# Seven twice-split products with other buffers and another order of their side work, in a gated mix of local attention and a GeGLU layer

## The chip, the cores and the metric

The kernel runs on one core of one Trainium2 chip. The metric is the device time of one execution in microseconds (us). Three executions of the kernel before took 753.84, 754.22 and 755.27 us; the median is 754.22. One more execution was taken with the hardware profiler on.

The core's engines run side by side, each through its own queue of instructions: TensorE (PE in the profile) multiplies matrices into eight banks of PSUM, VectorE (DVE) and ScalarE (ACT) work elementwise and can read and write PSUM, GpSimd (POOL) and SyncE (SP) mostly issue transfers (DMAs) here. PEld is PE's loading of weights.

## The reference

The input x has 2048 tokens of 1024 numbers (bfloat16). Two layers read it, and a gate per token mixes them:

```python
g = sigmoid((x * gate_w).sum(-1, keepdims=True))
a = attention(x, wqkv) @ wo          # 32 heads of 32, each token sees 8 tokens, 2 apart
b = (gelu(x @ w_gate) * (x @ w_up)) @ w_down      # 3584 hidden columns
return g * a + (1 - g) * b
```

## The kernel before, in words

The kernel splits its large matrix products by Strassen's method in Winograd's form: a product of two 2 by 2 block matrices is made from seven block products instead of eight, for some additions of blocks. An order written out by hand sets every engine's queue: inside `tc.manual_schedule` each engine runs its instructions in the order in which the program issues them, and the framework adds the semaphore waits that data, buffers and PSUM banks need.

The change lies in the last stage, after about 514 us. There the two output projections are one product. The hidden columns h of the GeGLU layer, times 1 - g, and the attention's output o, which already carries g, are laid side by side along the contraction: 28 tiles of h and 8 of o, each 128 deep, make 36. `w_down` and `wo` are stacked likewise. For each half s of the tokens (s = 0 and 1, 1024 tokens each) the left matrix A has two chunks of 512 tokens and two halves of the contraction of 18 tiles (`NK`); the right matrix R has two halves of the contraction and two halves of the 1024 output columns. A block is 18 tiles of 128 by 512, 18 KB in each partition. `R_BUF` cuts the arena in SBUF into ten buffers of that size; `plan[s]` gives each named block its buffer, and a buffer is used again and again.

The seven block products of one s, in the order of PE's queue (`down`), are P1 = A11 R11, P2 = A12 R21, P5 = S T1, P6 = S2 T2, P3 = (A12 - S2) R22, P7 = (A11 - A21) T3 and P4 = A22 T4, with S = A21 + A22 and S2 = A22 - (A11 - A21). The blocks T1 to T4 are differences of the weights, made earlier and kept in device memory (`t_d`). An A block is loaded (`load_A`), its h tiles are multiplied by 1 - g on DVE (`scale_task`, L894), and the sums are made there (`comb_task`, L901, five additions for a block). The difference A11 - A21 is written over A11, S2 over A21.

PE makes a plain block product with 72 matmuls of 512 columns (`mm`, L1015). Seven of the fourteen are split a second time (`level2`, matmuls L990 of 256 columns, 126 for a product): P5, P6 and P7 of s = 0, and P1, P5, P6 and P7 of s = 1. Such a product needs eight "forms" on DVE (`forms_L`, L959, and `forms_R`, L967, four each, written into two buffers named L5, R5 and so on), and consists of seven sub-products, each for two banks. Its four banks are XT (6, 7, 0, 1) or VT (2, 3, 4, 5), two groups of four. The sub-products add onto what stands in the banks, so the left halves are filled with zeros first (`zero_left`, L979, DVE). Between sub-products ScalarE copies half banks (L995): after the first one from one bank to another, before the second adds onto the same bank; after the third into float32 space `p5d` that lies behind the three right forms in their buffer. Ahead of the last sub-product DVE adds `p5d` to the right halves (L1003, the inner additions), first to the last two banks, then to the first two:

```python
            prod(0, 1, lf[:, 3], rq(1, 1))
            for i in (1, 0):
                TT(out=two_banks(bk, i, 1), in0=two_banks(bk, i, 1), in1=p5d, op=ALU.add)
            prod(1, 0, lq(1, 1), rf[:, 2])
```

After P1, four copies on ScalarE take its banks to `u2` (L1034, or L1048 and L1050 for s = 0); after P2 four take the first output (L1057); after P5 four take its banks to `qs` (L1066). After P6 DVE makes sums from the banks, `u2` and `qs` (L1074 and L1075); the other outputs are made by `add_out` (L1024), and `emit` sends each (L1020) by Pool's queue or, at the very end, SP's. The loads are issued on SP's queue, which holds a load until its buffer is free.

The last stage begins while the stage before it ends. PE starts P1 of s = 0 with the tiles that are there. The h tiles of A11 and A12 that come from the last two pairs of hidden columns are loaded by themselves, in `pre_down_3`, after Pool has stored these pairs to device memory (`h_store`, L256). SP then loads A21 (`loads(0, "A21")`), A22, T1 and T2.

Of the kernel before, what the change touches and what calls it, by code (L numbers as in the profile page):

```python
# [9 lines left out]
ALU = mybir.AluOpType  # L10
# [57 lines left out]
def kernel(  # L68
# [64 lines left out]
    with tc.manual_schedule(engines={mybir.EngineType.PE, mybir.EngineType.DVE, mybir.EngineType.Activation,  # L133
# [55 lines left out]
        def flat(a):  # L189
            return a.rearrange("p a b -> p (a b)")  # L190
# [609 lines left out]
        bufs = [reg3(R_BUF[k], NK, SC) for k in range(10)]  # L800
        NH_ = NPAIR

        def load_A(b, s, half, c, i0, i1, with_o):
            t0 = s * SUP + c * SC
            nc.sync.dma_start(out=b[:, i0:i1, :], in_=h_src(half, t0, i0, i1))
            if with_o:
                nc.sync.dma_start(out=b[:, NH_:NK, :], in_=o_d[:, half * 4:half * 4 + 4, t0:t0 + SC])

        def h_src(half, t0, i0, i1):
            return h_d[:, :, t0:t0 + SC].rearrange("p (i two) s -> p i two s", two=2)[:, i0:i1, half, :]  # L810
# [51 lines left out]
        def tf_close():  # L862
            while tf_open[0] and not tft.done:
# [4 lines left out]

        at_end(TFE - 1, tf_close)

        plan = [dict(A11=4, R11=5, A12=2, R21=3, A21=6, A22=0, S=8, T1=1, T2=9, L5=7, R5=5, L6=3, R6=1,
                     R22=7, T3=5, T4=8, L7=3, R7=1),
                dict(A11=6, R11=9, L1=2, R1=7, A12=4, R21=5, A21=3, A22=0, S=8, T1=1, T2=9, L5=2, R5=7, L6=5, R6=1,
                     R22=7, T3=2, T4=8, L7=5, R7=1)]
        u2 = regf(R_U2, 4 * SC).rearrange("p (j n) -> p j n", j=4)
        qs = regf(R_QS, 4 * SC).rearrange("p (j n) -> p j n", j=4)
        on = [0]
# [53 lines left out]
        def pre_down_3(s):  # L931
            B = Bs(s)
            for k, half in (("A11", 0), ("A12", 1)):
                load_A(B[k], s, half, 0, NE_, NH_, False)

        def loads(s, *names):
            B = Bs(s)
# [36 lines left out]
        def two_banks(bk, i, h):  # L974
            return banks[:, bk[2 * i]:bk[2 * i] + 2, h * HN:(h + 1) * HN]

        def zero_left(bk):
            for i in range(2):
                V.memset(two_banks(bk, i, 0), 0.0)  # L979

        def level2(bk, L, R, lf, rf):
            p5d = flat(rf)[:, 3 * KH * HN:3 * KH * HN + 4 * HN].bitcast(F32).rearrange("p (j n) -> p j n", j=2)
            lf, rf = quads(lf), quads(rf)
            lq, rq = lambda r, c: quarter(L, c, r), lambda r, c: quarter(R, r, c)
            c = lambda i, h, j: banks[:, bk[2 * i + j], h * HN:(h + 1) * HN]

            def prod(i, h, l, r, then=None):
                for j in range(2):
                    for kt in range(KH):
                        nc.tensor.matmul(c(i, h, j), lhsT=l[:, kt, j * P:(j + 1) * P], rhs=r[:, kt, :], start=False,  # L990
                                         stop=(kt == KH - 1), skip_group_check=True)
                    if then:
                        then(j)

            cp = lambda d, s_: nc.scalar.copy(out=d, in_=s_)  # L995
            prod(0, 0, lq(0, 0), rq(0, 0), lambda j: cp(c(1, 1, j), c(0, 0, j)))
            prod(0, 0, lq(0, 1), rq(1, 0))
            prod(1, 0, lf[:, 0], rf[:, 0], lambda j: cp(p5d[:, j, :], c(1, 0, j)))
            prod(1, 1, lf[:, 1], rf[:, 1], lambda j: cp(c(0, 1, j), c(1, 1, j)))
            prod(1, 1, lf[:, 2], rq(0, 1), lambda j: cp(c(1, 0, j), c(1, 1, j)))  # L1000
            prod(0, 1, lf[:, 3], rq(1, 1))
            for i in (1, 0):
                TT(out=two_banks(bk, i, 1), in0=two_banks(bk, i, 1), in1=p5d, op=ALU.add)  # L1003
            prod(1, 0, lq(1, 1), rf[:, 2])

        def down(s):
            B = Bs(s)
            last = s == 1
            eng = nc.gpsimd
            base = s * SUP  # L1010
            XT, VT = (6, 7, 0, 1), (2, 3, 4, 5)

            def mm(ps, L, R, j, start, q0=0, q1=NK):
                for q, i in list(enumerate(KORD))[q0:q1]:
                    nc.tensor.matmul(ps, lhsT=L[:, i, j * P:(j + 1) * P], rhs=R[:, i, :], start=(start and q == 0),  # L1015
                                     stop=(q == NK - 1), skip_group_check=not start)

            def emit(ot, c, nh, j):
                r0 = base + c * SC + j * P
                (nc.sync if last and (c, nh) == (1, 0) else eng).dma_start(out=o2[r0:r0 + P, nh * SC:(nh + 1) * SC], in_=ot)  # L1020

            def add_out(ps, t_, c, nh, j):
                ot = out_tile()
                TT(out=ot, in0=ps, in1=t_, op=ALU.add)  # L1024
                emit(ot, c, nh, j)

            A11, A12, A21, A22, S = B["A11"], B["A12"], B["A21"], B["A22"], B["S"]
            XP = [bank(XT[j]) for j in range(4)]
            VP = [bank(VT[j]) for j in range(4)]
            if last:  # L1030
                run(scale_task(A12, s, 0, 0, NE_))
                level2(XT, A11, B["R11"], B["L1"], B["R1"])
                for j in range(4):
                    nc.scalar.copy(out=u2[:, j, :], in_=XP[j])  # L1034
                loads(s, "T2")
                run(scale_task(A21, s, 1, 0, NE_))
            else:
                rest = scale_task(A21, s, 1, 0, NE_)
                for j in range(4):
                    if j > 1:  # L1040
                        mm(XP[j], A11, B["R11"], j, True)
                    else:
                        mm(XP[j], A11, B["R11"], j, True, 0, NK - 2)
                        yield
                        if j == 1:
                            for jj in range(2):
                                mm(XP[jj], A11, B["R11"], jj, True, NK - 2, NK)
                                nc.scalar.copy(out=u2[:, jj, :], in_=XP[jj])  # L1048
                    if j > 1:
                        nc.scalar.copy(out=u2[:, j, :], in_=XP[j])  # L1050
                    take(rest, 3)
                run(rest)
            run(comb_task(A11, A11, A21, ALU.subtract), scale_task(A22, s, 1, 0, NE_), comb_task(S, A21, A22, ALU.add))
            for j in range(4):
                mm(XP[j], A12, B["R21"], j, False)
                ot = out_tile()
                nc.scalar.copy(out=ot, in_=XP[j])  # L1057
                emit(ot, 0, 0, j)
            zero_left(VT)
            run(woven(forms_L(B["L5"], S), forms_R(B["R5"], B["T1"])))  # L1060
            run(comb_task(A21, A22, A11, ALU.subtract))
            S2 = A21
            zero_left(XT)
            level2(VT, S, B["T1"], B["L5"], B["R5"])
            for j in range(4):
                nc.scalar.copy(out=qs[:, j, :], in_=VP[j])  # L1066
            loads(s, "R22", "T3", "T4")
            run(woven(forms_L(B["L6"], S2), forms_R(B["R6"], B["T2"])))
            run(comb_task(A12, A12, S2, ALU.subtract))
            level2(XT, S2, B["T2"], B["L6"], B["R6"])  # L1070
            if not last:
                loads(1, "A11", "R11")
            for j in range(4):
                TT(out=u2[:, j, :], in0=XP[j], in1=u2[:, j, :], op=ALU.add)  # L1074
                TT(out=qs[:, j, :], in0=qs[:, j, :], in1=u2[:, j, :], op=ALU.add)  # L1075
            zero_left(XT)
            rest = woven(forms_L(B["L7"], A11), forms_R(B["R7"], B["T3"]))
            for j in range(4):
                mm(VP[j], A12, B["R22"], j, False)
                take(rest, 2)  # L1080
                add_out(VP[j], u2[:, j, :], 0, 1, j)
            run(rest)
            rest = pieces()
            if not last:
                N = Bs(1)
                run(scale_task(N["A11"], 1, 0, 0, NE_))
                rest = woven(forms_L(N["L1"], N["A11"]), forms_R(N["R1"], N["R11"]))
                take(rest, 2)
            level2(XT, A11, B["T3"], B["L7"], B["R7"])
            if not last:  # L1090
                loads(1, "A12", "R21", "A21", "T1")
            for j in range(4):
                add_out(XP[j], qs[:, j, :], 1, 1, j)
                TT(out=u2[:, j, :], in0=XP[j], in1=u2[:, j, :], op=ALU.add)
            if not last:
                zero_left(XT)
            for j in range(4):
                mm(VP[j], A22, B["T4"], j, True)
                take(rest, 2)
                add_out(VP[j], u2[:, j, :], 1, 0, j)  # L1100
            if not last:
                loads(1, "A22")
            run(rest)

        n = len(units)
        at(n - 16, lambda: load_R(Bs(0)["R11"], 0, 0))
# [73 lines left out]
```

## Time and profile before

| what | us |
|---|---|
| executions, median (lowest to highest) | 754.22 (753.84 to 755.27) |
| the profiled execution | 755.15 |
| its span, first to last instruction | 753.3 |
| PE busy in the span | 722.1 (96%) |
| DVE busy | 661.3 (88%) |
| ScalarE busy | 310.6 (41%) |
| Pool busy | 116.9 (16%) |
| mean granted clock of PE | 0.986 |

A busy PE is not PE at its peak; what a stage can win is read from PE's idle time there and from what ended it. The last stage by PE's timeline, start of each block product in us of the span:

| s | P1 | P2 | P5 | P6 | P3 | P7 | P4 | end |
|---|---|---|---|---|---|---|---|---|
| 0 | 516.5 (with gaps) | 543.4 | 559.24 | about 576.3 | 592.81 | 608.35 | 622.11 | 637.8 |
| 1 | 637.65 | 651.40 | 668.87 | about 688.3 | 704.81 | 720.35 | 734.10 | 749.8 |

In the tables of the profile, L followed by a number is a line of the kernel, an engine's name is followed by its operation and by the tile that it writes and the one that it reads, and a bracket gives the idle time before the instruction and the instruction or transfer that ended it.

### The profile page before, as it was taken

The page shows a single profiled execution, that of the slowest core. Times are in us where ns is not written, and L with a number is a line of the kernel's source. Part 1 is how long each engine was busy: PE and PEld are TensorE (multiplying, and loading weights), DVE is VectorE, ACT ScalarE, POOL GpSimd, SP SyncE. Part 2 cuts the span into 40 slices and gives each one's busy share as a digit, 9 for nine tenths or more (in the row PEclk, how much of TensorE's full clock was granted, in tenths as well). Part 3 has the DMA queues.
Part 4 walks back from the last instruction along what each step waited for, and adds up shares of the span by engine and source line. Part 5 has one row for each costly group of instructions (what it writes and reads, how often), then busy time and mean ns, then how long its engine had stood idle before and what let it go on. Part 6 is the DMA issues. An engine that isn't in the chain of part 4 may idle for free.

```text
span 753.3 us, 10346 instructions
## 1 busy us (share of the span) xinstructions
PE 722.1 (96%) x3945; PEld 394.5 (52%) x3945; DVE 661.3 (88%) x716; ACT 310.6 (41%) x556; POOL 116.9 (16%) x208
## 2 busy tenths in 40 slices
PE   8999999999999999999999999998698999997998
PEld 4466565555544444444444444443257675765673
DVE  3699999969998999999999999996399989699953
ACT  4544445445575755555555555552112010222010
POOL 1233435211201401011010000001010002000010
PEclk9999999999999999999999999999799999998999
DMA  9976864572337945345247652617966839932701
GB/s 279 265 213 223 259 198 145 211 233 84 105 93 223 364 149 161 123 140 170 84 155 228 195 170 71 208 57 245 361 273 219 320 117 319 384 135 97 288 22 57
DMA packets 119602, 143.92 MB, mean 191 GB/s; under 512 B 18897, under 2 KB 103025, under 8 KB 118529
## 3 DMA queue, kind: packets, MB, share of 16 engines
q1 hardware_dynamic: 105664, 102.58, 42.2%
q0 software_dynamic: 13600, 40.16, 15.7%
q8 instruction: 31, 0.51, 0.3%
q10 hardware_dynamic: 288, 0.52, 0.2%
q14 instruction: 19, 0.15, 0.1%
HBM read 101.16 MB, written 39.99 MB: 187 GB/s over the span
## 4 chain that ended last, share of the span: by engine, by line
PE 58%; DVE 15%; DMA 5%; issue 1%; ACT 1%; SPq 0%; DVEq 0%; ACTq 0%
PE banks L362 44%; PE banks L1015 9%; DVE arena L901 5%; PE banks L990 4%; DMA arena<-h_d 4%; DVE arena L967 3%; DVE arena L959 3%; DVE arena L894 1%; DMA arena<-in_B_w_down_dram 1%; DVE arena L593 1%; DVE arena L399 1%; DVE banks L979 1%; DVE banks L1003 0%; PE banks L598 0%; DVE arena L644 0%
## 5 line engine op out<-in xcount | busy, mean ns | idle before, releaser
L362 PE MATMUL banks<-arena 128*128 128x512 bf16 x2184 | 475.4, 379 | 4.8 <-DVE arena L399 3.0
L362 PEld LDWEIGHTS <-arena 128*128 128x128 bf16 x2184 | 240.5, 111 | 239.1 <-issue 11.0
L1015 PE MATMUL banks<-arena 128*128 128x512 bf16 x504 | 112.1, 384 | 8.6 <-DMA arena<-h_d 8.6
L990 PE MATMUL banks<-arena 128*128 128x256 bf16 x882 | 101.7, 279 | 11.6 <-DVE banks L1003 9.8
L399 DVE TENSOR_TENSOR arena<-banks,arena 128x1024 bf16<-128x1024 f32 x78 | 95.3, 1221 | 18.8 <-PE banks L362 11.7
L990 PEld LDWEIGHTS <-arena 128*128 128x128 bf16 x882 | 88.2, 100 | 25.6 <-issue 12.5
L385 ACT COPY arena<-banks 128x512 f32<-128x512 f32 x78 | 45.8, 587 | 130.8 <-PE banks L362 130.8
L1015 PEld LDWEIGHTS <-arena 128*128 128x128 bf16 x504 | 49.7, 99 | 68.8 <-DMA arena<-h_d 9.1
L370 ACT CAST arena<-banks 128x512 bf16<-128x512 f32 x102 | 59.8, 586 | 43.8 <-PE banks L362 43.8
L739 DVE TENSOR_TENSOR arena<-arena 128x2048 bf16<-128x2048 bf16 x64 | 77.1, 1220 | 0.5
L593 DVE TENSOR_TENSOR arena<-arena 128x2048 bf16<-128x2048 bf16 x64 | 74.8, 1219 | 0.1
L746 DVE TENSOR_TENSOR arena<-arena 128x2048 bf16<-128x2048 bf16 (+2 forms) x96 | 73.9, 776 | 1.0
L256 POOL DMA_DIRECT2D h_d<-arena x28 | 20.0, 716 | 251.5 <-DVE arena L252 205.2
L392 ACT COPY banks<-banks 128x512 f32<-128x512 f32 x78 | 44.5, 571 | 23.9 <-PE banks L362 18.1
L995 ACT COPY banks<-banks 128x256 f32<-128x256 f32 x42 | 15.0, 357 | 87.9 <-PE banks L990 87.9
L380 ACT COPY banks<-banks 128x512 f32<-128x512 f32 x78 | 45.0, 577 | 13.8 <-PE banks L362 12.7
L1020 POOL DMA_DIRECT2D out_dram<-arena x28 | 15.2, 543 | 197.6 <-DVE arena L1024 137.3
L901 DVE TENSOR_TENSOR arena<-arena 128x2048 bf16<-128x2048 bf16 (+1 forms) x40 | 41.9, 1120 | 0.0
L319 DVE TENSOR_TENSOR arena<-arena 128x1024 bf16<-128x1024 bf16 x60 | 38.7, 686 | 0.5
L894 DVE TENSOR_TENSOR arena<-arena,omgrep 128x2048 bf16<-128x2048 bf16 x24 | 27.9, 1221 | 12.2 <-DMA arena<-h_d 12.2
L368 ACT ACTIVATE arena<-banks 128x512 bf16<-128x512 f32 x54 | 32.3, 597 | 15.4 <-PE banks L362 15.4
L252 DVE TENSOR_TENSOR arena<-arena 128x2048 bf16<-128x2048 bf16 x28 | 34.1, 1217 | 5.0 <-ACT arena L370 3.7
(85 smaller groups left out, 441.4 us busy)
## 6 DMA issues: line engine op xcount, KB each, us to landing
arena<-t_d SPq DMA_DIRECT2D x8, 2304.0 KB, 14.6
h_d<-arena POOLq DMA_DIRECT2D x28, 512.0 KB, 4.0
arena<-in_B_w_down_dram SPq DMA_DIRECT2D x6, 1792.0 KB, 12.6
arena<-h_d SPq DMA_DIRECT2D x6, 1792.0 KB, 12.8
t_d<-arena POOLq DMA_DIRECT2D x36, 256.0 KB, 4.1
arena<-in_B_w_down_dram SPq DMA_DIRECT2D x32, 256.0 KB, 5.5
arena<-in_B_w_gate_dram SPq DMA_DIRECT2D x15, 512.0 KB, 5.4
arena<-in_B_w_up_dram SPq DMA_DIRECT2D x15, 512.0 KB, 4.5
```

Source lines behind the costliest of these rows:

```text
L362: self.pe = nc.tensor.matmul(ps, lhsT=self.L[form](kt), rhs=rhs[:, kt, :], start=(start and kt == 0), stop=(kt == HK - 1), skip_group_chec ...
L370: nc.scalar.copy(out=o_, in_=i_)
L380: nc.scalar.copy(out=self.Y, in_=self.X)
L385: nc.scalar.copy(out=self.p5s, in_=self.V)
L392: nc.scalar.copy(out=self.Z, in_=self.Y)
L399: TT(out=self.T[:, :, c2s], in0=pair, in1=self.p5s.rearrange("p (o n) -> p o n", o=1).to_broadcast([P, 2, SC]), op=ALU.add)
L593: TT(out=dst, in0=q.rearrange("p (o s) -> p o s", o=1).to_broadcast([P, NWIN, AC]), in1=_win_ap(k, [[-DIL, NWIN], [1, AC]]), op=ALU.mult)
L739: TT(out=prod2[(t // 2) % 2][:, t % 2], in0=ab, in1=_win_ap(v[:, t, HALO:HALO + AC], [[SJ, NJ], [-DIL, NWIN], [1, SJ]]), op=ALU.mult)
L746: TT(out=out_, in0=h(0), in1=h(1), op=ALU.add)
L901: TT(out=f(o_), in0=f(a), in1=f(b), op=op)
L990: nc.tensor.matmul(c(i, h, j), lhsT=l[:, kt, j * P:(j + 1) * P], rhs=r[:, kt, :], start=False, stop=(kt == KH - 1), skip_group_check=True)
L1015: nc.tensor.matmul(ps, lhsT=L[:, i, j * P:(j + 1) * P], rhs=R[:, i, :], start=(start and q == 0), stop=(q == NK - 1), skip_group_check=not ...
```

## The change

Four things are changed in the last stage, and `plan` is written anew for them.

- The difference A11 - A21 gets a buffer of its own, AD, and is made right behind the scaling of A21; P7 and S2 read it there. In s = 1 this comes ahead of the inner additions of P1.
- The inner additions leave `level2` and become `joins`, called later: after P5 behind all eight forms of P6; after P6 behind A12 - S2; after P7 of s = 0 behind the scaling and all forms of the next half's P1. They still come ahead of whatever reads the banks.
- `zero_left` runs on ScalarE: a copy of some finite numbers with a factor of zero. VT is filled before P2, XT right after the four copies of P2, ahead of P5.
- The two small loads of `pre_down_3` go to Pool's queue. The loads for s = 1 come in the order A12, A21, R21, A22, T1 instead of A12, R21, A21, T1, A22.

```diff
-        def load_A(b, s, half, c, i0, i1, with_o):
+        def load_A(b, s, half, c, i0, i1, with_o, eng=nc.sync):
...
-            nc.sync.dma_start(out=b[:, i0:i1, :], in_=h_src(half, t0, i0, i1))
+            eng.dma_start(out=b[:, i0:i1, :], in_=h_src(half, t0, i0, i1))
...
-        plan = [dict(A11=4, R11=5, A12=2, R21=3, A21=6, A22=0, S=8, T1=1, T2=9, L5=7, R5=5, L6=3, R6=1,
-                     R22=7, T3=5, T4=8, L7=3, R7=1),
-                dict(A11=6, R11=9, L1=2, R1=7, A12=4, R21=5, A21=3, A22=0, S=8, T1=1, T2=9, L5=2, R5=7, L6=5, R6=1,
-                     R22=7, T3=2, T4=8, L7=5, R7=1)]
+        plan = [dict(A11=4, R11=5, A12=2, R21=3, A21=6, A22=0, T1=1, T2=9, S=8, AD=7, L5=4, R5=5, L6=3, R6=1,
+                     R22=4, T3=8, T4=5, L7=3, R7=1),
+                dict(A11=6, R11=9, L1=2, R1=4, A12=7, R21=3, A21=8, A22=1, T1=5, T2=4, S=6, AD=0, L5=9, R5=2, L6=3, R6=5,
+                     R22=9, T3=6, T4=2, L7=3, R7=5)]
...
-                load_A(B[k], s, half, 0, NE_, NH_, False)
+                load_A(B[k], s, half, 0, NE_, NH_, False, nc.gpsimd)
...
         def zero_left(bk):
             for i in range(2):
-                V.memset(two_banks(bk, i, 0), 0.0)
+                nc.scalar.activation(out=two_banks(bk, i, 0), in_=omgrep[:, 0:SC].rearrange("p (a b) -> p a b", a=2),
+                                     func=ACT.Copy, scale=0.0)
...
+        def joins(bk, rf):
+            for i in range(2):
+                TT(out=two_banks(bk, i, 1), in0=two_banks(bk, i, 1), in1=part5(rf), op=ALU.add)
...
             prod(0, 1, lf[:, 3], rq(1, 1))
-            for i in (1, 0):
-                TT(out=two_banks(bk, i, 1), in0=two_banks(bk, i, 1), in1=p5d, op=ALU.add)
             prod(1, 0, lq(1, 1), rf[:, 2])
...
                 level2(XT, A11, B["R11"], B["L1"], B["R1"])
+                run(scale_task(A21, s, 1, 0, NE_), comb_task(AD, A11, A21, ALU.subtract))
+                joins(XT, B["R1"])
                 for j in range(4):
                     nc.scalar.copy(out=u2[:, j, :], in_=XP[j])
                 loads(s, "T2")
-                run(scale_task(A21, s, 1, 0, NE_))
             else:
-                rest = scale_task(A21, s, 1, 0, NE_)
+                rest = pieces(scale_task(A21, s, 1, 0, NE_), comb_task(AD, A11, A21, ALU.subtract))
...
-            run(comb_task(A11, A11, A21, ALU.subtract), scale_task(A22, s, 1, 0, NE_), comb_task(S, A21, A22, ALU.add))
+            zero_left(VT)
+            run(scale_task(A22, s, 1, 0, NE_), comb_task(S, A21, A22, ALU.add))
...
-            zero_left(VT)
+            zero_left(XT)
             run(woven(forms_L(B["L5"], S), forms_R(B["R5"], B["T1"])))
-            run(comb_task(A21, A22, A11, ALU.subtract))
+            run(comb_task(A21, A22, AD, ALU.subtract))
             S2 = A21
-            zero_left(XT)
             level2(VT, S, B["T1"], B["L5"], B["R5"])
+            run(woven(forms_L(B["L6"], S2), forms_R(B["R6"], B["T2"])))
+            joins(VT, B["R5"])
             for j in range(4):
                 nc.scalar.copy(out=qs[:, j, :], in_=VP[j])
             loads(s, "R22", "T3", "T4")
-            run(woven(forms_L(B["L6"], S2), forms_R(B["R6"], B["T2"])))
             run(comb_task(A12, A12, S2, ALU.subtract))
             level2(XT, S2, B["T2"], B["L6"], B["R6"])
             if not last:
                 loads(1, "A11", "R11")
+            joins(XT, B["R6"])
...
-            rest = pieces()
             if not last:
                 N = Bs(1)
                 run(scale_task(N["A11"], 1, 0, 0, NE_))
-                rest = woven(forms_L(N["L1"], N["A11"]), forms_R(N["R1"], N["R11"]))
-                take(rest, 2)
-            level2(XT, A11, B["T3"], B["L7"], B["R7"])
+                run(woven(forms_L(N["L1"], N["A11"]), forms_R(N["R1"], N["R11"])))
+            level2(XT, AD, B["T3"], B["L7"], B["R7"])
+            joins(XT, B["R7"])
             if not last:
-                loads(1, "A12", "R21", "A21", "T1")
+                loads(1, "A12", "A21", "R21", "A22")
...
             if not last:
-                loads(1, "A22")
-            run(rest)
+                loads(1, "T1")
```

More of the change, by code (lines that the diff above doesn't have):

```diff
@@ L978, in zero_left, with part5 @@
             for i in range(2):
-                V.memset(two_banks(bk, i, 0), 0.0)
+                nc.scalar.activation(out=two_banks(bk, i, 0), in_=omgrep[:, 0:SC].rearrange("p (a b) -> p a b", a=2),
+                                     func=ACT.Copy, scale=0.0)
+        def part5(rf):
+            return flat(rf)[:, 3 * KH * HN:3 * KH * HN + 4 * HN].bitcast(F32).rearrange("p (j n) -> p j n", j=2)
+        def joins(bk, rf):
+            for i in range(2):
+                TT(out=two_banks(bk, i, 1), in0=two_banks(bk, i, 1), in1=part5(rf), op=ALU.add)
         def level2(bk, L, R, lf, rf):
-            p5d = flat(rf)[:, 3 * KH * HN:3 * KH * HN + 4 * HN].bitcast(F32).rearrange("p (j n) -> p j n", j=2)
+            p5d = part5(rf)
             lf, rf = quads(lf), quads(rf)
@@ L1025, in add_out @@
                 emit(ot, c, nh, j)
-            A11, A12, A21, A22, S = B["A11"], B["A12"], B["A21"], B["A22"], B["S"]
+            A11, A12, A21, A22, S, AD = (B[k] for k in ("A11", "A12", "A21", "A22", "S", "AD"))
             XP = [bank(XT[j]) for j in range(4)]
@@ L1076, in down @@
             zero_left(XT)
-            rest = woven(forms_L(B["L7"], A11), forms_R(B["R7"], B["T3"]))
+            rest = woven(forms_L(B["L7"], AD), forms_R(B["R7"], B["T3"]))
             for j in range(4):
@@ L1098, in down @@
                 mm(VP[j], A22, B["T4"], j, True)
-                take(rest, 2)
                 add_out(VP[j], u2[:, j, :], 1, 0, j)
             if not last:
-                loads(1, "A22")
-            run(rest)
+                loads(1, "T1")
         n = len(units)
```

## The prediction

> **What bounds the kernel now.** I read the page's chain of waits first: PE holds 58% of it, DVE 15%, DMA 5%. DVE's share lies almost wholly after 520 us, in the last stage, which is all that the diff touches. So I read that stage from PE's timeline. A line gives start, length, instructions, and the idle time before it with its releaser.
>
> ```profile
> 516.53 3.62 PE L1015 MATMUL banks<-arena 128*128 128x512 bf16 x16
> ...
> 533.05 26.36 PE L1015 MATMUL banks<-arena 128*128 128x512 bf16 x112 [8.58 <-DMA arena<-h_d]
> ```
> ```profile
> 574.36 15.58 PE L990 MATMUL banks<-arena 128*128 128x256 bf16 x126 [3.17 <-DVE banks L1003]
> 590.85 2.13 PE L990 MATMUL banks<-arena 128*128 128x256 bf16 x18 [0.90 <-DVE banks L1003]
> ...
> 608.35 13.92 PE L990 MATMUL banks<-arena 128*128 128x256 bf16 x126
> ...
> 668.87 12.23 PE L990 MATMUL banks<-arena 128*128 128x256 bf16 x108 [1.77 <-DVE banks L979]
> 686.36 16.05 PE L990 MATMUL banks<-arena 128*128 128x256 bf16 x126 [5.25 <-DVE banks L1003]
> 702.85 2.12 PE L990 MATMUL banks<-arena 128*128 128x256 bf16 x18 [0.44 <-DVE banks L1003]
> ```
> An undisturbed split product is 126 matmuls in 13.76 us by the chain of waits (1.97 per sub-product), a plain one 72 in 15.54. PE idles 3.17 + 0.90 (P5 and P6 of s = 0) and 1.77 + 5.25 + 0.44 (s = 1), 11.5 us, all for DVE; 15.58 and 16.05 against 13.92 show restarts after idling that cost 1.65 and 2.1. So about 15.3 us could be won here.
>
> Next, DVE around the first of these waits, then ScalarE (ACT) there.
>
> ```profile
> 567.39 5.24 DVE L901 TENSOR_TENSOR arena<-arena 128x2048 bf16<-128x2048 bf16 x5
> 572.74 1.03 DVE L979 MEMSET banks<- 128x512 f32 x2
> 573.66 1.25 DVE L1003 TENSOR_TENSOR banks<-banks,arena 128x512 f32<-128x512 f32 x2
> 574.80 1.36 DVE L959 TENSOR_TENSOR arena<-arena 128x2304 bf16<-128x2304 bf16 x1
> ```
> ```profile
> 574.94 1.07 ACT L1066 COPY arena<-banks 128x512 f32<-128x512 f32 x2 [5.26 <-DVE banks L1003]
> 576.19 0.59 ACT L1066 COPY arena<-banks 128x512 f32<-128x512 f32 x1 [0.17 <-PE banks L990]
> 578.11 0.59 ACT L1066 COPY arena<-banks 128x512 f32<-128x512 f32 x1 [1.33 <-PE banks L990]
> 579.17 0.36 ACT L995 COPY banks<-banks 128x256 f32<-128x256 f32 x1 [0.48 <-PE banks L990]
> ```
> DVE does not idle from 539.05 to the last addition at 590.8: it is the bound of this stretch, and the additions come when its queue reaches them. ACT runs the four copies of P5 out of PSUM (L1066) before the first inner copy of P6 (L995), as the program has them.
>
> **The change part by part.** All sums are against the profiled execution: 755.15 us, span 753.3, so 1.85 around it; the median of the three runs, 754.22, is 0.93 lower.
>
> *A difference A11 - A21 in its own buffer.* Same five additions (5.14 us). At s = 0 it wins nothing: DVE passes from scaling to it at 542.46 unheld. At s = 1 it and the scaling of A21 (3.4) can run beside P1 instead of behind it; counted below.
>
> *Zero fills on ScalarE.* DVE loses 14 of 0.485 us, a pair with its gap 1.1; two pairs lie on DVE's chain in each half: -2.1 there. ACT's price for one is not shown; the nearest rows, its 128x512 copies, take 0.57 to 0.59 (357 ns for 256 columns is the lower end, 1.05 for 1024 the upper). The VT fill lies in ACT time that is idle. The XT fill comes just before P5's first inner copies and holds them 0.4 to 0.8 us; P5 has 9.8 us of slack (below), so it costs nothing; without that cover, 0.4.
>
> *Additions behind the next forms.* P5's last sub-product no longer waits for them, so P5 runs through: at s = 0 from 559.24 to 573.0. But the copies L1066 wait for the additions, which now wait for all eight forms of P6, and behind these copies in ACT's queue stand P6's inner copies. PE's second sub-product of P6 adds onto the bank that the first inner copy must read. So PE can do one sub-product of P6 and then waits for: forms, additions, four copies, inner copy.
>
> s = 0, from the landing of A21 at 539.05: scale, difference, scale A22, S: 17.19 (539.05 to 556.24); forms of P5 10.12 (557.37 to 567.49); S2 5.14; forms of P6 10.14 (574.90 to 585.04); gaps 0.1: 581.75. First addition 0.57, 582.3. Four copies 2.05 (L1034's four at 650.37), 584.4. Inner copy 0.36: PE goes on at 584.8, idle since 575.0. Six sub-products 11.8, restart 2.1: P6 ends at 598.7, against 592.98 now (590.85 + 2.13): **+5.7**. The 9.8 us wait replaces 3.17 + 0.90. The forms of P6 fill T1's buffer, free after P5's fifth sub-product at 569.1; DVE arrives at 572.8, so nothing is added. T4's load now waits for the late additions (582.9), but is used 40 us later.
>
> The restart's price is from the rows after 533.05: ten matmuls take 4.2 us there, 0.43 each instead of 0.216, with 0.50 in the granted-clock column until 536; 2.0 to 2.1 lost, and 1.65 after the 3.17 us wait. The Trainium skill ("TensorE: Matmul & The Clock Gate", part 1) says that PE runs at half clock for about 3.4 us after an idle window of that length. An estimate from that page is 1.7, and the sum by it is 0.4 lower; the rows decide, and both are in the range.
>
> Everything after s = 0's P6 is PE's: additions and sums (6.4), forms of P7 with four outputs (12.5) lie beside P3; A11's scaling (3.4) and P1's eight forms (10.1) beside P7. The additions of P7 come 2.7 us after its end but free banks that are needed 13 us later.
>
> s = 1, from P, the end of P4 (637.81 now). Loads are issued from P7's end, P - 15.5. Now the fourth, T1, lands 32.4 later (639.43 + 14.9), and A22, fifth, at 659.57 = P + 21.8, which DVE waits for. In the new order A12, A21, R21, A22, A22's h part is fourth: 25.6 for three (A21's o part, 633.63 + 13.8) plus 5.2 for 1.79 of 2.36 MB: P + 15.3. DVE: last output 0.65, scale A12 3.4, A21 3.4, difference 5.14, the second addition behind P1's last sub-product: free at P + 14.4, so A22 is still what it waits for, by 0.9. The copies behind P1's first addition (P + 13.2) end at P + 13.85, as P1 ends: no new wait. Then 3.4 + 5.14 + 10.12 + 5.14 + 10.14 with 0.2 of gaps: P + 49.4; addition, copies, inner copy 3.0: P + 52.4; 11.8 + 2.1: P6 ends at P + 66.4, against 704.97 = P + 67.16: **-0.8**. If A22 came early enough, DVE's own time gives -1.7.
>
> *Two small loads on Pool's queue.* They are issued when the store of pair 13 has landed (515.77 + 8.2 = 524.0), two issues of up to 0.71, and the last store (524.68) goes behind them, 1.4 later; its data is wanted 70 us later. Loads of 256 KB on SP take 8.7 there; Pool's stores under the same load 6.8 for 512 KB. So PE may go on at 529 to 533. That ends nothing: the waits above hang on A21's landing. SP issues A21 1.4 us earlier, but the transfer engines are full (share 1.1, 350 to 390 GB/s from 522 on) and the bytes ahead are the same. Bounds: 1.3 us earlier (512 KB less in its queue) to 0.3 later; I take 0.3 earlier, near none, because Pool's stores are served among SP's data. **-0.3**. The Trainium skill ("DMA: Bandwidth & Descriptors", queues, rings and completion order) has each transfer engine go round its queues packet by packet; by that the two loads take their share at once and A21's landing stays, so its sum would be 0.3 higher. No run here shows a load on Pool's queue in this place.
>
> Sum: 5.7 - 0.8 - 0.3 = **+4.6**: span 757.9, that execution 759.75, against the median 754.22 + 4.6 = 758.8 us.
>
> **The rivals.**
> *ScalarE is not held (faster).* P6's inner copies need no result of the additions; if they got past the four waiting copies, all waits of 11.5 and the restarts of 3.75 would go: 754.2 - 15.3 = 738.9. Against it: the L1066 lines all come before L995. It decides if PE's wait inside P6 is under 5 us.
> *A21 lands much earlier.* Each us earlier takes one off s = 0's chain. If it landed when the small loads land now (533.6, 5.4 earlier): 758.8 + 0.3 - 5.4 = 753.7, no change; from 6.1 earlier than now it is faster. Against it: the full transfer engines.
> *The second half is later still.* A22 does not gain from the new order and lands at P + 21.8: 6.5 more, 765; or P5 ends late and holds the forms in T1's buffer (0.9 us to spare at s = 1: P + 39.6 against 40.5), some 761 to 762. For it: four loads in one queue that drains at 370 GB/s; against: 7 MB ahead instead of 9.
>
> **How the numbers follow.** Forecast 0.72, ScalarE not held 0.08, early A21 0.08, late second half 0.12. The forecast's own range: low, A21 1.3 early, A22 early (-1.7), restart 1.65: 756.4; high, A21 0.3 late, no gain at s = 1, a us for queues: 760.9. The range 753.5 to 762.5 takes in early A21 and half of the late case, and leaves out some 0.16. About 0.2%, 1.5 us, is what a measurement can tell from no change: faster 0.10 (first rival, a quarter of the second), same 0.07, slower 0.83.
>
> **What the new profile would show.** PE: no wait inside P5; one of 9 to 10 us in s = 0's P6 after 18 or so matmuls, released by an inner copy, and one of 6 to 7 in s = 1. ACT idle before L1066 for the additions. DVE: no fills, the additions right behind eight forms. A21 landing at 538 to 539, A22 at P + 15. The prediction falls if PE runs through P6, or if A21 lands before 535.

## The result and the profile after

The changed kernel takes 761.33 us (median; 760.44 to 761.44), the kernel before 754.53 beside it: a ratio of 1.0087, 95% interval 1.0070 to 1.0105. It is 6.8 us slower. The profiled execution took 761.44 us with a span of 759.7, 6.4 more than the span before.

PE's timeline after, from the first wait to the end of P6 in s = 1 (start, length, instructions, idle time before and its releaser). Lines have moved: the inner products are L998, the plain ones L1021, the inner copies L1003, the additions L987, the copies of P5 L1075.

```profile
531.12 25.95 PE L1021 MATMUL banks<-arena 128*128 128x512 bf16 x112 [6.47 <-DMA arena<-h_d]
556.92 16.04 PE L998 MATMUL banks<-arena 128*128 128x256 bf16 x144
585.09 13.86 PE L998 MATMUL banks<-arena 128*128 128x256 bf16 x108 [12.13 <-ACT banks L1003]
598.78 15.70 PE L1021 MATMUL banks<-arena 128*128 128x512 bf16 x72
...
643.62 13.92 PE L998 MATMUL banks<-arena 128*128 128x256 bf16 x126
657.74 15.70 PE L1021 MATMUL banks<-arena 128*128 128x512 bf16 x72 [0.21 <-ACT arena L1042]
673.28 16.04 PE L998 MATMUL banks<-arena 128*128 128x256 bf16 x144
696.99 14.22 PE L998 MATMUL banks<-arena 128*128 128x256 bf16 x108 [7.67 <-ACT banks L1003]
711.04 15.70 PE L1021 MATMUL banks<-arena 128*128 128x512 bf16 x72
```

The five waits for DVE are gone; a small one of 0.21 us, for P1's copies, is new ahead of P2 in s = 1. P5 and the first sub-product of P6 run as one piece, 126 + 18 = 144 matmuls, and then PE stands for 12.13 us in s = 0 and 7.67 in s = 1, both times for ScalarE's first inner copy of P6. What holds that copy is seen on ScalarE, and what holds ScalarE on DVE.

```profile
567.15 0.36 ACT L1003 COPY banks<-banks 128x256 f32<-128x256 f32 x1 [0.63 <-PE banks L998]
582.71 2.05 ACT L1075 COPY arena<-banks 128x512 f32<-128x512 f32 x4 [15.20 <-DVE banks L987]
584.62 0.69 ACT L1003 COPY banks<-banks 128x256 f32<-128x256 f32 x2
```
```profile
566.51 5.23 DVE L901 TENSOR_TENSOR arena<-arena 128x2048 bf16<-128x2048 bf16 x5
571.82 1.36 DVE L959 TENSOR_TENSOR arena<-arena 128x2304 bf16<-128x2304 bf16 x1
...
580.71 1.35 DVE L967 TENSOR_TENSOR arena<-arena 128x2304 bf16<-128x2304 bf16 x1
581.98 1.29 DVE L987 TENSOR_TENSOR banks<-banks,arena 128x512 f32<-128x512 f32 x2
```

DVE makes S2, then the eight forms of P6, then the additions at 581.98. ScalarE has done nothing for 15.20 us, runs its four copies out of P5's banks, and only then the inner copies that PE wants. DVE is nearly as busy as before (655.0 us against 661.3); what counts is the order of its queue.

By s: P3 of s = 0 starts at 598.78 instead of 592.81, 5.97 later. From there to the start of P1 of s = 1 takes 44.84 us in both kernels. From that start (643.62, called P below; the prediction counts from the end of P4, here 643.78) to the next P3 it takes 67.42 instead of 67.16, 0.26 more. The tail behind P4 is 0.16 longer. Together 6.4, the whole difference of the spans.

### The profile page after: what moved, and what is told of

Same layout as the page of the kernel before. It is cut to its first block, busy times and chain, and to the rows that moved or that the text cites. A ratio compares the mean times of both kernels' runs of the same rounds, so it can differ in the third digit from the quotient of the medians.

```text
span 759.7 us, 10371 instructions
## 1 busy us (share of the span) xinstructions
PE 722.4 (95%) x3945; PEld 395.0 (52%) x3945; DVE 655.0 (86%) x702; ACT 317.5 (42%) x570; POOL 118.3 (16%) x210
## 5 line engine op out<-in xcount | busy, mean ns | idle before, releaser
L998 PE MATMUL banks<-arena 128*128 128x256 bf16 x882 | 101.9, 279 | 19.8 <-ACT banks L1003 19.8
L1021 PE MATMUL banks<-arena 128*128 128x512 bf16 x504 | 111.7, 383 | 6.7 <-DMA arena<-h_d 6.5
L998 PEld LDWEIGHTS <-arena 128*128 128x128 bf16 x882 | 88.3, 100 | 33.6 <-issue 20.5
L1021 PEld LDWEIGHTS <-arena 128*128 128x128 bf16 x504 | 49.6, 99 | 66.7 <-DMA arena<-h_d 7.0
L959 DVE TENSOR_TENSOR arena<-arena 128x2304 bf16<-128x2304 bf16 x28 | 37.9, 1354 | 0.4
## 6 DMA issues: line engine op xcount, KB each, us to landing
arena<-in_B_w_down_dram SPq DMA_DIRECT2D x6, 1792.0 KB, 12.9
```

## The experiments

The theory: P6 waits through ScalarE's queue for the additions that stand behind P6's forms on DVE. The main rival: P6 waits for its own operands (forms in T1's buffer, late transfers), so that buffers, load order or fills carry the loss. All times are medians, with the ratio to the kernel before, run beside them, and its 95% interval; "now" and "changed" mean the changed kernel, 761.33.

**1. P5's copies behind P6's inner copies.** The additions stay where the change put them.

```diff
             joins(VT, B["R5"])
-            for j in range(4):
-                nc.scalar.copy(out=qs[:, j, :], in_=VP[j])
...
             level2(XT, S2, B["T2"], B["L6"], B["R6"])
+            for j in range(4):
+                nc.scalar.copy(out=qs[:, j, :], in_=VP[j])
```

> The changed kernel, with one thing moved: the four copies of P5 into qs stand behind P6's inner copies in ScalarE's queue; the inner additions of P5 stay behind all forms of P6. Theory (ScalarE's queue: P6's inner copies are held by the four copies, and these by the late additions): PE runs through P6 in both halves, P6 of s = 0 ends near 587 instead of 598.8, P6 of s = 1 ends 57 us after P4 of s = 0 instead of 67.4; 12.0 + 10.4 = 22 us less, 739. Rival (P6 waits for its own operands: forms in T1's buffer, or late transfers): PE waits in P6 as before, 761. If only part of the wait goes, both act.

Measured: 741.05 us, 0.9823 (0.9804 to 0.9843). PE's timeline of this kernel:

```profile
532.36 26.67 PE L1021 MATMUL banks<-arena 128*128 128x512 bf16 x110 [6.39 <-DMA arena<-h_d]
558.87 27.92 PE L998 MATMUL banks<-arena 128*128 128x256 bf16 x252
586.63 15.70 PE L1021 MATMUL banks<-arena 128*128 128x512 bf16 x70
...
647.39 15.70 PE L1021 MATMUL banks<-arena 128*128 128x512 bf16 x70 [2.01 <-ACT arena L1042]
662.93 27.82 PE L998 MATMUL banks<-arena 128*128 128x256 bf16 x252
```

P5 and P6 are one piece of 252 matmuls in both halves, without a wait. The additions are as late as in the changed kernel and the forms lie in the same buffers, so neither the additions as such nor the operands of P6 make these two waits: ScalarE's order does. Of the 22 us expected, 20.3 came; 2.01 went into a wait in s = 1 for P1's copies (run 8).

**2. P5's additions and copies ahead of P6's forms.**

```diff
             level2(VT, S, B["T1"], B["L5"], B["R5"])
-            run(woven(forms_L(B["L6"], S2), forms_R(B["R6"], B["T2"])))
             joins(VT, B["R5"])
             for j in range(4):
                 nc.scalar.copy(out=qs[:, j, :], in_=VP[j])
+            run(woven(forms_L(B["L6"], S2), forms_R(B["R6"], B["T2"])))
```

> The changed kernel with the inner additions of P5 and its four copies ahead of P6's forms instead of behind them; all else stays. Theory (late additions through ScalarE's queue): the additions run as P5 ends (571.7 to 573.6), the copies end near 575, and P6 runs with the forms close ahead of it, ending near 588 in s = 0 and 58 us after P4 in s = 1: about 20 less, 741. Rival (P6 waits for forms or transfers): the forms come 1.9 us later than now, so PE waits as long or longer, 761 to 763.

Measured: 740.73 us, 0.9817 (0.9798 to 0.9836). PE waits 1.31 us for the inner copy in s = 0's P6; in s = 1 it waits 0.28 for the copy and 0.17 for a form. Though the forms come later than in the changed kernel, they are almost in time. The rival's 761 to 763 falls.

**3. The kernel before with P5's additions late, and nothing else.**

```diff
-        def level2(bk, L, R, lf, rf):
+        def level2(bk, L, R, lf, rf, inner=True):
...
-            for i in (1, 0):
+            for i in (1, 0) if inner else ():
...
-            level2(VT, S, B["T1"], B["L5"], B["R5"])
+            level2(VT, S, B["T1"], B["L5"], B["R5"], False)
+            run(woven(forms_L(B["L6"], S2), forms_R(B["R6"], B["T2"])))
+            joins(VT, B["R5"])
             for j in range(4):
                 nc.scalar.copy(out=qs[:, j, :], in_=VP[j])
             loads(s, "R22", "T3", "T4")
-            run(woven(forms_L(B["L6"], S2), forms_R(B["R6"], B["T2"])))
```

> The kernel before, with one part of the change alone: the inner additions of P5 and its four copies behind the forms of P6 (old buffers, old loads, zero fills on DVE, additions of the other products where they were). Theory (late additions through ScalarE's queue): DVE reaches the additions 10.1 us later, PE goes on in P6 at about 587 in s = 0 and P6 ends 7.8 us later in each half: 15.6 more than the kernel before, 770. Rival (new buffers, load order or fills on ScalarE carry the loss): no loss here, 754 or less.

Measured: 770.75 us, 1.0218 (1.0199 to 1.0238): 16.1 more than the kernel before, where 15.6 was expected. The two waits are there with the old buffers, the old loads and the fills on DVE:

```profile
586.40 14.23 PE L995 MATMUL banks<-arena 128*128 128x256 bf16 x108 [11.51 <-ACT banks L1000]
...
705.88 14.22 PE L995 MATMUL banks<-arena 128*128 128x256 bf16 x108 [10.81 <-ACT banks L1000]
```

So this one move costs 16.1 us by itself. In the changed kernel 6.8 are left of it, so the other parts together win 9.3 beside it.

**4. The small loads back on SP's queue.**

```diff
-                load_A(B[k], s, half, 0, NE_, NH_, False, nc.gpsimd)
+                load_A(B[k], s, half, 0, NE_, NH_, False)
```

> The changed kernel with the two small loads of A11 and A12 back on SP's queue. Prediction's step: PE goes on after its first wait some 2 us later (533 instead of 531.1), A21 lands at the same time within 0.3 us, and the time stays within 0.5 us, 761. Rival (the loads on Pool's queue help or hurt the chain): A21's landing moves by 1.3 us or more and the time with it.

Measured: 761.8 us, 1.0096 (1.0080 to 1.0111), the same as the changed kernel within the intervals. PE's lines:

```profile
533.26 26.70 PE L1021 MATMUL banks<-arena 128*128 128x512 bf16 x110 [8.43 <-DMA arena<-h_d]
...
585.30 13.87 PE L998 MATMUL banks<-arena 128*128 128x256 bf16 x108 [9.47 <-ACT banks L1003]
```

PE goes on 2.1 us later after its first wait and stands 2.7 less in P6; it goes on there at 585.30 instead of 585.09. DVE starts on A21 at 539.25 instead of 539.06, in an execution that reached P1 0.17 later. The time won by Pool's queue was only waited out later.

**5. The fills back on DVE.**

```diff
-                nc.scalar.activation(out=two_banks(bk, i, 0), in_=omgrep[:, 0:SC].rearrange("p (a b) -> p a b", a=2),
-                                     func=ACT.Copy, scale=0.0)
+                V.memset(two_banks(bk, i, 0), 0.0)
...
-            zero_left(VT)
             run(scale_task(A22, s, 1, 0, NE_), comb_task(S, A21, A22, ALU.add))
...
-            zero_left(XT)
+            zero_left(VT)
             run(woven(forms_L(B["L5"], S), forms_R(B["R5"], B["T1"])))
...
             S2 = A21
+            zero_left(XT)
```

> The changed kernel with the zero fills back on DVE, at the places of the kernel before (VT ahead of P5's forms, XT behind S2). By the prediction's working two pairs lie on DVE's chain to P5's additions in each half, 1.05 to 1.1 us a pair: P6 of s = 0 ends 2.1 later, P6 of s = 1 another 2.1, 4.2 more than the changed kernel, 765.6. Rival (the fills are beside other work on either engine): 761.

Measured: 765.12 us, 1.0138 (1.0121 to 1.0154), 3.8 more than the changed kernel where 4.2 was expected. The change takes 14 fills of 0.485 us from DVE. Eight of them, two pairs in each half, lie on the chain to P6's waits, and these are worth about their length, 3.9 us. PE goes on in P6 1.9 us later in s = 0 and 1.6 in s = 1, counted from the start of each half's P1.

**6. A22 of s = 1 behind T1.**

```diff
-                loads(1, "A12", "A21", "R21", "A22")
+                loads(1, "A12", "A21", "R21")
...
-                loads(1, "T1")
+                loads(1, "T1", "A22")
```

> The changed kernel with A22 of s = 1 loaded behind T1 again. T1's buffer is free only when P4 of s = 0 ends (P), so A22 lands near P + 22 instead of P + 16.0. If A22's landing starts the chain that ends in P6's wait in s = 1, as the profile after shows (DVE idle 1.24 for it), P6 there ends 6 us later: 767. If DVE's own work sets it, or the forms wait for T1, the time moves less than 2 us: 761 to 763.

Measured: 765.96 us, 1.0149 (1.0134 to 1.0165), 4.6 more. DVE's wait for A22 grows to 6.04 us:

```profile
663.99 3.50 DVE L894 TENSOR_TENSOR arena<-arena,omgrep 128x2048 bf16<-128x2048 bf16 x3 [6.04 <-DMA arena<-h_d]
```

That is P + 20.8 (P = 643.22), 4.8 later than in the changed kernel, and P6 ends at P + 71.7, 4.3 later. A22's landing does start the chain of s = 1. The size was expected too large: SP was still pushing R21 until 644, so T1, whose buffer came free at 643.2, was held by almost nothing.

**7. All inner additions back inside the products**, so that the other parts of the change stand alone.

```diff
             prod(0, 1, lf[:, 3], rq(1, 1))
+            for i in (1, 0):
+                TT(out=two_banks(bk, i, 1), in0=two_banks(bk, i, 1), in1=p5d, op=ALU.add)
             prod(1, 0, lq(1, 1), rf[:, 2])
...
-                joins(XT, B["R1"])
...
-            joins(VT, B["R5"])
...
-            joins(XT, B["R6"])
...
-            joins(XT, B["R7"])
```

> The changed kernel with the inner additions of all split products back inside the product, ahead of its last sub-product, as in the kernel before: what is left is the other parts of the change. Theory (the additions' new place carries the whole loss, the other parts gain): P6 of s = 0 ends near 590.6 (598.8 now, 592.98 in the kernel before), P6 of s = 1 at P + 64.5 (67.4 now): 11 less than the changed kernel, 750, under the kernel before. Rival (other parts lose too): 754.5 or more.

Measured: 755.46 us, 1.0010 (1.0001 to 1.0020): not the 750 expected. P6 came out as worked out (P3 of s = 0 starts at 591.07, expected 590.6; P6 of s = 1 ends at P + 64.3, expected 64.5). The rest is a wait that the expectation had not seen, in P7 of s = 0:

```profile
606.61 11.95 PE L998 MATMUL banks<-arena 128*128 128x256 bf16 x108
621.97 3.79 PE L998 MATMUL banks<-arena 128*128 128x256 bf16 x18 [3.40 <-DVE banks L1011]
```

The change puts all eight forms of the next half's P1 ahead of P7 in the program. With P7's additions inside the product they stand behind these forms on DVE: 3.40 us of wait and 1.66 in the slow restart (3.79 instead of 2.13).

**8. P5's copies behind P6's inner copies (run 1), and P1's additions in s = 1 behind three pieces of the difference instead of five.**

```diff
-                run(scale_task(A21, s, 1, 0, NE_), comb_task(AD, A11, A21, ALU.subtract))
-                joins(XT, B["R1"])
+                run(scale_task(A21, s, 1, 0, NE_))
+                ad = comb_task(AD, A11, A21, ALU.subtract)
+                take(ad, 3)
+                joins(XT, B["R1"])
+                run(ad)
```

> The kernel with P5's copies behind P6's inner copies, and in s = 1 P1's inner additions behind three of the five pieces of A11 - A21 instead of all five. In the run with the copies moved, PE waits 2.01 us for P1's copies ahead of P2 in s = 1, since outputs that wait for their stores make DVE late. The split should take that wait away: 739. If DVE's lateness is not what holds the copies, 741.

Measured: 738.02 us, 0.9783 (0.9768 to 0.9797). PE's wait ahead of P2 is 0.19 us instead of 2.01. This is the fastest version: 16.7 us under the kernel before.

**9. R21 of s = 0 loaded behind A21.**

```diff
-            load_R(B["R21"], 1, 0)
...
-            loads(0, "A21")
+            loads(0, "A21", "R21")
```

> The changed kernel with R21 of s = 0 loaded behind A21 instead of ahead of it; nothing else. It moves A21's landing alone: 2.3 MB fewer lie ahead of it, so it should land near 531.5 instead of 539.06, and R21 near 539, 2 us ahead of its use. Theory (in s = 0 the wait in P6 hangs on DVE's chain from A21's landing, us for us): P6 of s = 0 ends 7.5 us earlier, 591.3; time 754. Rival (something else, such as T1's buffer or PE's own products, holds P6): less than half of that, 758 or more.

Measured: 764.49 us, 1.0124 (1.0107 to 1.0141): 3.2 more instead of 7.5 less. DVE's timeline and PE's line:

```profile
537.29 3.50 DVE L894 TENSOR_TENSOR arena<-arena,omgrep 128x2048 bf16<-128x2048 bf16 x3 [8.63 <-DMA arena<-h_d]
540.70 5.23 DVE L901 TENSOR_TENSOR arena<-arena 128x2048 bf16<-128x2048 bf16 x5
550.78 3.50 DVE L894 TENSOR_TENSOR arena<-arena,omgrep 128x2048 bf16<-128x2048 bf16 x3 [4.86 <-DMA arena<-h_d]
```
```profile
588.27 14.62 PE L997 MATMUL banks<-arena 128*128 128x256 bf16 x108 [11.49 <-ACT banks L1002]
```

The run did not move A21's landing alone, and moved it little: A21 landed 1.8 us earlier, 2.7 counted from P1, which this execution reached 0.9 later, not 7.5. SP's queue shows a reason, first in the changed kernel, then here:

```profile
516.14 7.79 SPq L823 DMA_DIRECT2D arena<-in_A_wo_dram  x1
524.36 0.92 SPq L805 DMA_DIRECT2D arena<-h_d  x1
```
```profile
515.52 0.78 SPq L807 DMA_DIRECT2D arena<-o_d  x1
525.11 0.54 SPq L805 DMA_DIRECT2D arena<-h_d  x1
```

A21 (L805) is issued 7.6 us after the start of P1 in the changed kernel and 7.5 after it here: it reads h, and here SP stands 8.7 us for Pool's store of h to land. So A21 could not use the room that R21 left ahead of it. In the changed kernel, with R21 still under way, the transfer engines move 375 GB/s from 524 to 526.5; here they move next to nothing from 524.7 to 526.5. From issue to landing A21 takes 12.2 us instead of 14.7. R21, which now stands behind A21 in SP's queue, waits for the same store.

A22, now behind R21, landed so late that DVE waits a second time. The chain then starts from A22: its scaling begins at 550.78 instead of 547.61, 3.17 later, and PE goes on in P6 at 588.27 instead of 585.09, 3.18 later. The expected number failed; that P6 follows DVE's chain us for us is shown, in the other direction.

**10. Run 8 with R21 behind A21, and P1 of s = 0 as four parts of 16 tiles and then four tails of 2.**

```diff
-            load_R(B["R21"], 1, 0)
...
-            loads(0, "A21")
+            loads(0, "A21", "R21")
...
                 for j in range(4):
-                    if j > 1:
-                        mm(XP[j], A11, B["R11"], j, True)
...
+                    mm(XP[j], A11, B["R11"], j, True, 0, NK - 2)
+                    if j == 0:
                         yield
...
+                for j in range(4):
+                    mm(XP[j], A11, B["R11"], j, True, NK - 2, NK)
+                    nc.scalar.copy(out=u2[:, j, :], in_=XP[j])
```

> The kernel with P5's copies behind P6's inner copies and P1's additions split (738.0), and besides R21 of s = 0 behind A21, and P1 of s = 0 made as four parts of 16 tiles and then four tails of 2, so that PE works on 32 more matmuls (6.9 us) while it waits for the small loads. P1 should end near 533.5, P2 wait for R21 until about 539, and P6 of s = 0 end near 582 instead of 585: 735. If R21 lands later than 541, no gain: 738.

Measured: 741.99 us, 0.9831 (0.9816 to 0.9845), 4 more than run 8. PE's first wait shrinks to 2.22 us and a new one of 6.73 stands ahead of P2, for R21 at 543.13. R21 is issued at 525.86 only, behind A21, which again waits for the store of h (run 9).

**11. Run 7 with the forms of the next P1 back at their old places** (two ahead of P7, the others between P4's outputs).

```diff
-                run(woven(forms_L(N["L1"], N["A11"]), forms_R(N["R1"], N["R11"])))
+                rest = woven(forms_L(N["L1"], N["A11"]), forms_R(N["R1"], N["R11"]))
+                take(rest, 2)
...
                 mm(VP[j], A22, B["T4"], j, True)
+                take(rest, 2)
...
                 loads(1, "T1")
+            run(rest)
```

> The kernel with all inner additions inside the products (755.5), and the forms of the next half's P1 back at their old places: two ahead of P7, the others between the outputs of P4. In that kernel PE waited 3.40 us in P7 of s = 0 for additions that stood behind all eight forms in DVE's queue, and 18 matmuls then took 3.79 instead of 2.13. If these forms are the cause, 5 us go: 750.4. If not, 755.5.

Measured: 750.29 us, 0.9944 (0.9929 to 0.9959), as expected; PE's wait in P7 is gone. With the additions and P1's forms at their old places, the other parts of the change win 4 us; beside the late additions it was 9.3 (run 3).

**12. Run 8 with P1 in parts and tails alone** (the second half of run 10's diff).

> The kernel at 738.0 (P5's copies behind P6's inner copies, P1's additions split) with one more change: P1 of s = 0 is made as four parts of 16 tiles and then four tails of 2, so PE has 6.9 us of work during its first wait (6.5 us and a restart of 2). R21 and A21 are loaded as before. If DVE's chain from the landings of A21 and A22 sets the end of P6 in s = 0, PE only waits later (in P5 and P6) and P6 ends within 1.5 us of 585: 737 to 738. If PE's own work sets it, 6 to 8 us go: 731.

Measured: 740.06 us, 0.9798 (0.9785 to 0.9811): no gain over run 8. PE's lines:

```profile
521.36 27.79 PE L1021 MATMUL banks<-arena 128*128 128x512 bf16 x125
555.60 20.22 PE L998 MATMUL banks<-arena 128*128 128x256 bf16 x162 [6.45 <-DMA arena<-t_d]
...
587.12 15.70 PE L1021 MATMUL banks<-arena 128*128 128x512 bf16 x70
```

The first wait is filled, and 6.45 us come back ahead of P5, for T1. P6 ends at 587.12, 2.1 later than in run 8 (1.4 counted from P1), a little outside the 737 to 738 expected. PE's own work does not set this stretch: what it waits for are T1's landing and, in P6, two forms (0.32 and 0.41 us) and a copy (0.40).

## Why the prediction was right, point by point

- **The mechanism.** The prediction's central step, that P5's copies hold P6's inner copies because the additions stand behind eight forms, is what the trace shows and what runs 1 to 3 tell apart from the rivals. PE went on in s = 0's P6 at 585.09 where 584.8 was worked out. The waits were 12.13 and 7.67 us, where 9 to 10 and 6 to 7 were to be seen.
- **The term for s = 0** was +5.7 less 0.3 for the small loads, and measured +5.97. A21's landing did not move: 539.06 against 539.05 before. So the 0.3 that I took for SP's shorter queue was none, and the prediction's own reason against it held, that the bytes ahead are the same: A21 was issued 1.8 us earlier and took 14.7 us instead of 12.9. Run 4 has it at the same place with these loads on SP. (The executions differ by 0.2 us in when they reach P1, so less than that is not told apart.) The Trainium skill ("DMA: Bandwidth & Descriptors", queues, rings and completion order) let one expect that, and both landings agree; how the packets of the queues took turns, no trace here shows. The wait itself was 12.13 us, not 9.8, since PE came 2.3 earlier out of P2 by the small loads on Pool's queue; the prediction had said that this ends nothing, and run 4 shows it.
- **The term for s = 1** was the one mis-sized: -0.8 was predicted, +0.26 measured. Counted from the end of P4, as the prediction does, A22 landed at 15.8 (659.58 - 643.78), not 15.3; from there to PE's going on it took 37.4 us, not 37.1; and the six sub-products with their restart took 14.2 to P6's end instead of 13.9. The mechanism, a chain on DVE from A22's landing, is borne out by run 6.
- **The restart's price.** 2.1 was taken. Six sub-products took 13.69 us (598.78 - 585.09) in s = 0 and 14.05 (711.04 - 696.99) in s = 1, 1.9 and 2.25 more than the 11.8 of an undisturbed run. In twelve such restarts (the changed kernel and runs 3 to 6 and 9) it was 1.8 to 2.7, 2.2 on average, so 2.1 was a fair size. The granted clock in s = 0 reads 0.50 until 589, 3.9 us after PE went on. By the Trainium skill ("TensorE: Matmul & The Clock Gate", part 1) the prediction estimated 1.7, from about 3.4 us at half clock; the first restart lies halfway between 1.7 and 2.1, and all twelve lie above 1.7.
- **The fills on ScalarE.** -2.1 in each half; run 5 gives 3.8 for both.
- **The difference in its own buffer and the next P1's forms ahead of P7** cost next to nothing in the changed kernel, as predicted: P7 has no wait, and the 0.21 us ahead of P2 in s = 1, where "no new wait" was predicted, only shortens P6's wait. Once that wait is gone the difference does cost time, 2.01 us there in run 1, until run 8 splits it. Run 7 shows that the second is free only as long as P7's additions are late too.
- **The sum**, +4.6, was 1.8 short of the spans' 6.4 and 2.2 short of the medians' 6.8: 0.6 from s = 0, 1.1 from s = 1, 0.16 from the tail. 761.33 lies inside the range, but above the forecast's own upper bound of 760.9. That bound was added up 0.3 too low: 0.6 for A21 from 0.3 early to 0.3 late, 0.8 and 1 on top of 758.8 make 761.2.
- **The rivals.** "ScalarE is not held" fell with PE's wait of 12.13 us and ScalarE's of 15.20; made real by run 1, it was worth 20 us from the changed kernel and 13.6 from the one before, near the 15.3 named for it. "A21 lands much earlier" did not happen, and run 9 could not bring it about, since A21 waits for the store of h that it reads. Of "The second half is later still", A22 landed 0.5 us later than worked out, of the 6.5 named.

## What to carry to other kernels

An engine that runs its queue in order passes a wait on to everything behind it. When a step is moved later, look for who reads its result, and for what stands behind that reader in its queue: here four copies that nobody needed until P3, 14 us after the last of them, held two that the matrix engine needed at once, and one reordering on ScalarE turned a loss of 6.8 us into a gain of 13.6. Time that is won ahead of a wait that hangs on another engine's chain is only waited out later.

## What was not expected

- Moved work can be free beside one order and dear beside another. The next P1's forms, moved ahead of P7, cost nothing with late additions and 5.2 us with early ones (runs 7 and 11: 755.46 and 750.29).
- A load is held by what it reads as well as by what lies ahead of it. With R21 out of its way, A21 was issued no earlier, because it waits for Pool's store of h, and landed 1.8 us earlier instead of 7.5 (run 9). R21, issued 1.7 us behind it, took little of the difference: from A21's issue to its landing SP's queue moved 2.53 MB, of which A21 is 1.84 and its o part, issued next, up to 0.52, so R21 at most 0.7. Pool's queue moved 1.05 MB in that time, as in the changed kernel. How the rest of the difference divides between the idle transfer engines after the issue and their slower pace (293 GB/s until the landing, 361 in the changed kernel) stays open.
- T1, which PE and DVE do not wait for in the kernel before, lands at 554.8 in the changed kernel (issued at 539.86, 14.9 later), only 2.1 ahead of the start of P5; run 12, where PE came earlier, waited for it.
